# A tile's first four transposes on TensorE, written as two, three matmuls, and two

## The chip, the cores and the metric

The kernel runs on one core of one Trainium2 chip. The metric is the device time of one execution in microseconds; before the change the median of three runs is 2777.08 us (2773.55 to 2779.66).

## The reference

The program is a Fourier filter with soft thresholding, followed by a gated feed-forward block. `x` has 8 sequences of 3072 tokens with 256 features; the feed-forward width is 1536.

```python
X = np.fft.rfft(x, axis=1)
Yr = Xr @ w_r - Xi @ w_i + b_r
Yi = Xr @ w_i + Xi @ w_r + b_i
Yr = np.sign(Yr) * np.maximum(np.abs(Yr) - 0.01, 0.0)   # the same for Yi
y = np.fft.irfft(Yr + 1j * Yi, n=3072, axis=1)
xn = y / sqrt(mean(y * y, -1) + 1e-6) * rms_g           # 24576 tokens
g, val = xn @ w_gate, xn @ w_val
out = (g / (1 + exp(-g)) * val) @ w_out
```

## The kernel before, in words

The 24,576 tokens are cut into 48 tiles T = 0 to 47 of 512 tokens, six tiles to a sequence (a batch b). For each tile there are 12 steps, one per 128 columns of the feed-forward width, 576 steps in all. A step forms the gate and value products of the tile into the PSUM banks `g` and `v` (`straight`, L955, in the first three tiles; `products`, L979, in the other 45), goes through the Silu and the product with the value on ScalarE and VectorE, and adds its share of the output into the bank `acc` (`down`, L1014). Numbers are kept as a high and a low float32r part, so each product is three matmuls (high by high, high by low, low by high). That is why nearly every piece of TensorE's work in `products`, `down` and the Fourier part is three matmuls of 128x256 or a multiple of three; in `straight` it is twelve.

While batch b is worked off, the next sequence is filtered in the same program (`spectrum`): its Fourier units put matmuls into the bank `f` (names `pf`, `pm`, `pb`, L572 to L699), woven in between the steps of three of the tiles.

Before a tile's steps can begin, its 512 normalised tokens have to stand with the features on the partitions. `transposes` (L912) does this for one half h of the features: four TensorE transposes of 128x128 in plain float32 (`pt`, L917), one per 128 tokens, into one PSUM bank, which ScalarE then reads in one instruction (L931, into `xf`). h = 0 comes first and h = 1 some steps later. Both use the pool `f`, which has a single bank, and so do the Fourier units. So a tile has eight transposes, in two runs of four. `combine` then forms the operands of the tile's products on VectorE and ScalarE (L936 to L941).

The order of everything is made by a planner (`Plan`): each operation is recorded with a due time, the engines it can run on, a cost, and the names that it reads and writes (`op`). `schedule` simulates the engines several times forwards and backwards and returns the operations by their start; `emit` (L292) writes them out in that order. Within an engine that order is the program's order; the waits between engines follow from what is read and written. An operation on TensorE is one Python function and was always written out in one piece, though neighbouring operations can come from different steps.

Around one tile's transposes the trace's names are: `pt` the transposes, `acc` the output sums, `g` and `v` the gate and value products, `xf` the transposed tile before it is combined.

Of the kernel before, what the change touches and what calls it, by code (L numbers as in the profile page):

```python
# [127 lines left out]
class Plan:  # L128
# [61 lines left out]
    def schedule(self):  # L190
        ops = self.ordered()
        wrote, read, after = {}, {}, [[] for _ in ops]
        waits = [0] * len(ops)
        for i, (_, _, _, _, rs, ws) in enumerate(ops):

            one = tuple(t for t in rs if t in self.BANKS)
            rs, ws = tuple(t for t in rs if t not in one), ws + one
            deps = {wrote[t] for t in rs + ws if t in wrote} | {j for t in ws for j in read.get(t, ())}
            for j in deps:
                after[j].append(i)  # L200
            waits[i] = len(deps)
            for t in ws:
                wrote[t], read[t] = i, []
            for t in rs:
                read.setdefault(t, []).append(i)
        start, on = self.forward(ops, after, waits, [o[0] for o in ops], None)
        best = None
        for n in range(self.PASSES):
            late = self.backward(ops, after, start, on)
            start, on = self.forward(ops, after, waits, late, None if n % 4 == 3 else on)  # L210
            end = max(start)
            if best is None or end < best[0]:
                best = end, start, on
        _, start, on = best
        return [(ops[i][3], on[i]) for _, i in sorted(zip(start, range(len(ops))))]

    def lag(self, e, to):
        near = 0.0 if e == "P" else 0.06
# [71 lines left out]
        return late  # L290

    def emit(self):  # L292
        for fn, e in self.schedule():
            fn(e)


@with_exitstack
def fourier_glu_kernel(ctx: ExitStack, tc: tile.TileContext, x, w_r, w_i, b_r, b_i, wg, wv, wo, rg, tabs, units, tws, out):
# [3 lines left out]
    P = 128  # L302
# [35 lines left out]
    def f32(ap):  # L338
        return ap.bitcast(F32)
# [7 lines left out]
    def op(engines, cost, fn, r=(), w=()):  # L347
        plan.add(at[0], engines, cost, fn, [*r, *gate], w)

    def dve(n):  # L350
        return 0.09 + n / 990

    def act(n, more=0.0):
        return 0.1 + more + n / 1180
# [16 lines left out]
    class Room:  # L371


        def __init__(self, tag, shape, name, dt=F32):
            pool, n = POOLS[tag]
            k = turns[tag] = turns.get(tag, -1) + 1
            self.ring, self.k, self.n = tag, k, n
            self.tok = Tok(f"{tag}{k % n}")
            self.tok.room = self
            self.first = [self.tok, f"{tag}#"]  # L380
            self.args, self.t = (pool, shape, name, dt, tag), None
# [6 lines left out]
        def __call__(self):  # L388
            if self.t is None:
                pool, shape, name, dt, tag = self.args  # L390
                self.t = pool.tile(list(shape), dt, tag=tag, name=name)
            return self.t

    class Bank(Room):
# [9 lines left out]
        def flat(self):  # L404
            return self().rearrange("p a b -> p (a b)")
# [28 lines left out]
    def first(s, p, n=4, tag="t4"):  # L434
        x0, x1, x2 = ((lambda k=k: blk(s, k)()[:, p:p + n, :]) for k in range(3))
        s0, s1, s2 = (s.tok(*range(8 * k + p, 8 * k + p + n)) for k in range(3))
        t = Room(tag, (P, n, D), f"t4_{s.b}_{p}")
        add(n * D, lambda f: f(t(), x1(), x2(), ALU.add), s1 + s2, t.first)
        add(n * D, lambda f: f(x0(), x0(), t(), ALU.add), [t.tok], s0)

        def diff():
            add(n * D, lambda f: f(x1(), x1(), x2(), ALU.subtract), s2, s1)

        def rest():
            op("V", dve(n * D), lambda _: V.scalar_tensor_tensor(x2(), t(), -1.5, x0(), ALU.mult, ALU.add), [t.tok] + s0, s2)

        return diff, rest
# [464 lines left out]
    def transposes(get, toks, T, h, xn, xf):  # L912
        ps = Room("acc" if T == 0 and h else "f", (P, 4, P), f"pt{T}_{h}")

        def go(_):
            for i in range(4):
                PE.matmul(  # L917
                    ps()[:, i, :], lhsT=get(i)[:, h * P:(h + 1) * P], rhs=ident,
                    start=(i == 0), stop=(i == 3), is_transpose=True, skip_group_check=True,
                )  # L920

        flat = lambda: ps().rearrange("p a b -> p (a b)")
        op("P", 0.45, go, toks, ps.first)
        if xf is None:
            to = lambda lp: xn()[:, lp, 2 * h:2 * h + 2, :].rearrange("p a b -> p (a b)")
            op("A", act(512) + 0.09, lambda _: A.activation(to(0), flat(), AF.Copy, scale=rgs[:, h:h + 1]), [ps.tok, "rgs"], [xn.part(f"h{h}0")] + xn.first * (h == 0))
            w = [xn.part(f"h{h}1")] + ["ready"] * (T == 0 and h)
            op("V", dve(512) + 0.06, lambda _: V.scalar_tensor_tensor(to(1), flat(), rgs[:, h:h + 1], f32(to(0)), ALU.mult, ALU.subtract), [ps.tok, xn.part(f"h{h}0")], w)
            return
        to = lambda: xf()[:, 2 * h:2 * h + 2, :].rearrange("p a b -> p (a b)")  # L930
        op("A", act(512) + 0.09, lambda _: A.activation(to(), flat(), AF.Copy, scale=rgs[:, h:h + 1]), [ps.tok, "rgs"], [xf.tok] + xf.first * (h == 0))  # L931
# [155 lines left out]
    for p, tag in zip((0, 4, 2, 6), ("t4", "as", "xs", "t3")):  # L1087
        rest = first(s, p, 2, tag)
# [72 lines left out]
    for h in range(2):  # L1161
        transposes(lambda i: rows()[:, i, :], [f"{rows.tok}.{p}" for p in range(4)] + [rows.tok, "ident"], 0, h, xns[0], None)
# [110 lines left out]
    for b in range(B):  # L1273
# [6 lines left out]
        for t in range(NT):  # L1280
            T = b * NT + t
            for i in range(NF):
                n = NF * T + i
                if T:
                    at[0] = n - 3
                    if not plain(T):
                        trs[n] = fetch(0, i, Room("tr", (P, 2, 512), f"tr{n}", F32R))
                    else:
                        trs[n] = trs[n - 1] if i % 4 else fetch(2, i // 4, Room("tr", (P, 2, 512), f"tb{n}", F32R))
                    if NF <= n < NF * PLAIN and n % (PLAIN - 1) == 0:  # L1290
                        at[0] = n - 2.9
                        mixed_weights((n - NF) // (PLAIN - 1))
                    at[0] = n - 1
                    wo_s[n] = fetch(1, i, Room("wo", (P, 2, D), f"wo{n}", F32R))
                o = step(n, xns[T], i, not plain(T))
                if i == 0 and T + 1 < NT * B:
                    nb, nt = (b, t + 1) if t + 1 < NT else (b + 1, 0)
                    xns[T + 1] = Room("xn", (P, 2, 7, 256), f"xn{T + 1}", F32R)
                    xf = Room("xf", (P, 7, 256), f"xf{T + 1}") if not plain(T + 1) else None
                    for h in range(2):  # L1300
                        at[0] = NF * (T + 1) - 4 + h
                        transposes(
                            lambda i, nb=nb, nt=nt: seqs[nb]()[:, 4 * nt + i, :],
                            seqs[nb].tok(*range(4 * nt, 4 * nt + 4)), T + 1, h, xns[T + 1], xf,
                        )
                    if xf:
                        combine(T + 1, xns[T + 1], xf)
            at[0] = NF * (T + 1) + LATER - 0.95
            store(b, t, o)
# [31 lines left out]
```

## Time and profile before

| | us |
|---|---|
| median of three runs | 2777.08 |
| profiled execution, its own time | 2773.16 |
| its span, from the first to the last instruction | 2771.4 |
| TensorE matmuls (PE), busy | 2733.7 (99%) |
| weight loads (PEld), busy | 2720.0 (98%) |
| VectorE (DVE), busy | 2330.5 (84%) |
| ScalarE (ACT), busy | 1987.4 (72%) |

A matmul's recorded duration (279 ns) is its way through a pipeline; the next begins before it is done. The pace of TensorE is therefore read as a stretch's length divided by the number of matmuls in it, not from a busy share, which is full either way. A table by windows gives the length, the busy time and the count in brackets for each engine, and the clock that TensorE was granted (1.00 is 2.4 GHz). A window counts an instruction that only reaches into it, so each count is two to three too high.

### The profile page before, as it was taken

To read this page: it belongs to the slowest core of one execution; us is meant where nothing else is said; L and a number is where in the kernel's file an instruction comes from. 1 tells how busy PE (TensorE), PEld (TensorE's weight loads), DVE (VectorE), ACT (ScalarE), POOL (GpSimd) and SP (SyncE) were. 2 spreads that over 40 slices of the span, in tenths; PEclk is the share of its full clock that TensorE was granted. 3 is DMA by queue.
4 is the path that set the end of the run, shared out by engine and by line. 5 is a ranking of instruction groups with operands and counts; after the bars stand their busy time and mean duration, and the time that the engine had idled before them with its cause. 6 is when DMAs were issued, how large, how long until landed. Compare 5 with 4: busy or idle time off the path is not lost.

```text
span 2771.4 us, 60161 instructions
## 1 busy us (share of the span) xinstructions
PE 2733.7 (99%) x23321; PEld 2720.0 (98%) x23321; DVE 2330.5 (84%) x4063; ACT 1987.4 (72%) x4894; POOL 90.4 (3%) x177
## 2 busy tenths in 40 slices
PE   7899999999999999999999999999999999999999
PEld 6799999999999999999999999999999999999999
DVE  9989789987998779987899778997789887966665
ACT  5656678777877778777787777877778777776665
POOL 0000000000000000000000000000000000000000
PEclk9999999999999999999999999999999999999999
DMA  6476676676776667767686666866667666666665
GB/s 223 148 237 211 210 230 227 220 227 214 232 250 218 212 218 244 229 209 229 217 260 213 219 225 210 260 213 218 221 221 253 214 222 218 208 207 219 211 211 189
DMA packets 256112, 610.94 MB, mean 220 GB/s; under 512 B 24401, under 2 KB 81106, under 8 KB 255826
## 3 DMA queue, kind: packets, MB, share of 16 engines
q1 hardware_dynamic: 231634, 519.00, 56.6%
q0 software_dynamic: 24192, 88.09, 10.6%
q8 instruction: 183, 3.00, 0.4%
q14 instruction: 103, 0.84, 0.1%
HBM read 567.68 MB, written 39.32 MB: 219 GB/s over the span
## 4 chain that ended last, share of the span: by engine, by line
PE 97%; DVE 2%; DMA 1%; ACT 1%; issue 0%; SPq 0%; ACTq 0%; DVEq 0%
PE acc L1014 28%; PE v L979 27%; PE g L979 20%; PE pf L572 4%; PE pm L634 4%; PE pb L699 2%; PE pm L630 2%; PE v L955 2%; PE g L955 2%; PE pt L917 2%; PE pm L755 1%; PE pb L694 1%; PE pb L779 1%; PE pm L611 1%; PE pf L733 1%
## 5 line engine op out<-in xcount | busy, mean ns | idle before, releaser
L1014 PE MATMUL acc<-wo,hs 128*128 128x256 f32 x6912 | 1008.7, 279 | 2.2 <-DMA wo<-do 1.4
L1014 PEld LDWEIGHTS acc<-wo,hs 128*128 128x128 f32 x6912 | 891.5, 188 | 3.5 <-DMA wo<-do 1.6
L979 PE MATMUL v<-xn,tr 128*128 128x256 f32 x4860 | 785.4, 279 | 0.7 <-DVE y L992 0.7
L979 PEld LDWEIGHTS v<-xn,tr 128*128 128x128 f32 x4860 | 659.8, 188 | 1.3 <-DVE y L992 1.1
L979 PE MATMUL g<-xn,wb 128*128 128x256 f32 x3240 | 543.2, 279 | 0.8 <-ACT h L993 0.8
L992 DVE TENSOR_TENSOR y<-v,p 128x512 f32<-128x512 f32 x540 | 370.6, 686 | 115.7 <-PE v L979 108.3
L979 PEld LDWEIGHTS g<-xn,wb 128*128 128x128 f32 x3240 | 448.7, 188 | 1.0 <-ACT h L993 1.0
L1007 DVE TENSOR_TENSOR hs<-h,hs 128x512 fp32r<-128x512 f32 x576 | 394.4, 685 | 63.7 <-ACT hs L1006 59.3
L996 DVE TENSOR_TENSOR h<-h,y 128x512 f32<-128x512 f32 x540 | 369.7, 685 | 69.2 <-ACT h L995 66.5
L1006 ACT ACTIVATE hs<-h 128x512 fp32r<-128x512 f32 x576 | 362.1, 629 | 79.2 <-DVE h L996 41.8
L985 ACT ACTIVATE v<-g 128x256 f32<-128x256 f32 x540 | 200.4, 371 | 132.5 <-PE g L979 128.4
L988 ACT ACTIVATE v<-v 128x256 f32<-128x256 f32 x540 | 200.4, 371 | 109.3 <-PE v L979 106.1
L979 PE MATMUL g<-xn,tr 128*128 128x256 f32 x1620 | 276.1, 279 | 0.0
L979 PE MATMUL v<-xn,wb 128*128 128x256 f32 x1620 | 275.5, 279 | 0.0
L995 ACT ACTIVATE h<-v 128x256 f32<-128x256 f32 x540 | 206.5, 382 | 68.9 <-PE v L979 63.7
L993 ACT ACTIVATE h<-g 128x256 f32<-128x256 f32 x540 | 207.0, 383 | 66.8 <-PE g L979 54.2
L979 PEld LDWEIGHTS g<-xn,tr 128*128 128x128 f32 x1620 | 226.6, 188 | 0.0
L979 PEld LDWEIGHTS v<-xn,wb 128*128 128x128 f32 x1620 | 226.5, 188 | 0.0
L545 POOL DMA_DIRECT2D tab<-in_tabs_dram x168 | 89.4, 532 | 2259.6 <-PE v L979 973.4
L986 ACT ACTIVATE p<-g 128x256 f32<-128x256 f32 x296 | 112.7, 381 | 47.1 <-DVE y L992 45.4
L572 PE MATMUL pf<-tab,as 128*128 128x256 f32 x1008 | 137.5, 279 | 1.9 <-ACT as L564 1.5
L572 PEld LDWEIGHTS pf<-tab,as 128*128 128x128 f32 x1008 | 126.0, 189 | 2.3 <-ACT as L564 1.7
(172 smaller groups left out, 3529.8 us busy)
## 6 DMA issues: line engine op xcount, KB each, us to landing
tr<-dt SPq DMA_DIRECT2D x540, 512.0 KB, 4.0
wo<-do SPq DMA_DIRECT2D x564, 256.0 KB, 3.5
tab<-in_tabs_dram POOLq DMA_DIRECT2D x168, 512.0 KB, 4.8
out_dram<-o SPq DMA_DIRECT2D x32, 512.0 KB, 4.4
seq<-in_x_dram SPq DMA_DIRECT2D x28, 512.0 KB, 5.7
seq<-in_x_dram SPq DMA_DIRECT2D x25, 256.0 KB, 4.8
unit<-in_units_dram SPq DMA_DIRECT2D x12, 512.0 KB, 4.3
dt<-tw SPq DMA_DIRECT2D x12, 512.0 KB, 4.0
```

Of the source, the lines that this page charges most:

```text
L572: PE.matmul(ps[:, h, :], lhsT=r()[:, lp, ri, h * P:(h + 1) * P], rhs=f[:, rp, ri, :], start=(h + k + ri == 0), stop=(k == 2 and ri == 1), ...
L979: PE.matmul(dst(), lhsT=w(lp), rhs=xn()[:, rp, x, :], start=start and k == 0, stop=k == 2, skip_group_check=True)
L985: op("A", act(256), lambda _: A.activation(left(), p1(), AF.Copy), [one.tok], two.first)
L986: op("AV", {"A": act(256), "V": dve(256)}, lambda e: A.activation(p5(), p5_(), AF.Copy) if e == "A" else V.tensor_copy(p5(), p5_()), [one. ...
L988: op("A", act(256), lambda _: A.activation(right(), left(), AF.Copy), [], [two.tok])
L992: op("V", dve(512), lambda _: V.tensor_tensor(y(), two(), p5().unsqueeze(1).to_broadcast([P, 2, 256]), ALU.add), [two.tok, p5.tok], y.first)
L993: op("A", act(256), lambda _: A.activation(s()[:, :256], p1(), AF.Silu), [one.tok], s.first)
L995: op("A", act(256), lambda _: A.activation(s()[:, 256:], right(), AF.Silu), [two.tok], [s.part("b")])
L996: op("V", dve(512), lambda _: V.tensor_tensor(s(), s(), y().rearrange("p a b -> p (a b)"), ALU.mult), [y.tok, s.part("b")], [s.tok])
L1006: op("A", act(512), lambda _: A.activation(h()[:, 0], s(), AF.Copy), [s.tok], h.first)
L1007: add(512, lambda f: f(h()[:, 1], s(), f32(h()[:, 0]), ALU.subtract), [s.tok], [h.tok])
L1014: PE.matmul(o()[:, c, :], lhsT=h()[:, lp, c * P:(c + 1) * P], rhs=wo_()[:, rp, :], start=(i == 0 and k == 0 and c % 2 == 0), stop=(i == NF ...
```

## The change

`emit` learns to hold back part of an operation. An operation whose function is a `Halves` is written out as its first half; the rest is kept and written out right after the next TensorE operation, or sooner, if an operation comes up that touches the PSUM bank written, or that writes what the transposes read. `transposes` uses this for h = 0 of every tile but the first. The planner's order, its costs and the engines chosen are not touched; it still plans the four as one operation.

```diff
     def emit(self):
-        for fn, e in self.schedule():
-            fn(e)
+        rest = None
+        for (_, _, _, fn, reads, writes), e in self.schedule():
+            if rest and (rest[2] & {*reads, *writes} or rest[1] & {*writes}):
+                rest = rest[0](e)
+            after = fn(e)
+            if rest and e == "P":
+                rest = rest[0](e)
+            if isinstance(fn, Halves):
+                rest = after, {*reads}, {*writes}
+        assert rest is None
+
+class Halves:
+    def __init__(self, go, n):
+        self.go, self.n = go, n
+
+    def __call__(self, _):
+        self.go(0, self.n // 2)
+        return lambda _: self.go(self.n // 2, self.n)
...
     def transposes(get, toks, T, h, xn, xf):
-        def go(_):
-            for i in range(4):
+        def go(i0, i1):
+            for i in range(i0, i1):
...
-        op("P", 0.45, go, toks, ps.first)
+        op("P", 0.45, Halves(go, 4) if T and not h else lambda _: go(0, 4), toks, ps.first)
```

TensorE's order before, at a tile of the second batch (`pt_0` is h = 0, `pt_1` is h = 1, x is the number of instructions):

```order
L1014 MATMUL acc_5557<-wo_5692,hs_5647 128x256 x6
L917 MATMUL pt_0_5750<-ident,seq_1670 128x128 x4
L979 MATMUL v_5680<-xn_5212,tr_5593 128x256 x3
L979 MATMUL v_5755<-xn_5212,tr_5649 128x256 x3
L1014 MATMUL acc_5557<-wo_5692,hs_5647 128x256 x6
L917 MATMUL pt_1_5782<-ident,seq_1670 128x128 x4
```

The same place after the change (the lines stand 19 further down, and a name's number has moved by two):

```order
L1033 MATMUL acc_5557<-wo_5692,hs_5647 128x256 x6
L936 MATMUL pt_0_5750<-ident,seq_1670 128x128 x2
L998 MATMUL v_5680<-xn_5212,tr_5593 128x256 x3
L936 MATMUL pt_0_5750<-ident,seq_1670 128x128 x2
L998 MATMUL v_5753<-xn_5212,tr_5649 128x256 x3
L1033 MATMUL acc_5557<-wo_5692,hs_5647 128x256 x6
L936 MATMUL pt_1_5782<-ident,seq_1670 128x128 x4
```

One piece of three matmuls has gone ahead of the last two transposes of h = 0. This happens in 47 tiles; in one of them, in `straight`, the piece is twelve matmuls, in the other 46 it is three.

ScalarE's order before, at the same place:

```order
L801 ACTIVATE sq_7_5757,ssq_160<-seq_1670 128x256
L931 ACTIVATE xf_5766<-pt_0_5750,rgs 128x512
L988 ACTIVATE v_5755<-v_5755 128x256
L993 ACTIVATE h_5780<-g_5651 128x256
L1006 ACTIVATE hs_5787<-h_5701 128x512
L931 ACTIVATE xf_5766<-pt_1_5782,rgs 128x512
```

And after the change:

```order
L820 ACTIVATE sq_7_5755,ssq_160<-seq_1670 128x256
L950 ACTIVATE xf_5766<-pt_0_5750,rgs 128x512
L1007 ACTIVATE v_5753<-v_5753 128x256
L1012 ACTIVATE h_5780<-g_5651 128x256
L1025 ACTIVATE hs_5787<-h_5701 128x512
L950 ACTIVATE xf_5766<-pt_1_5782,rgs 128x512
```

Nothing moves on ScalarE, and nothing on VectorE, GpSimd or SyncE either; the first reading of `pt` (L931, now L950) waits for a transpose that stands three matmuls later.

## Rows read from the trace of the kernel before

**Rows 1.** The page: busy time of each engine, and the granted clock in 40 slices.
```profile
PE 2733.7 (99%) x23321; PEld 2720.0 (98%) x23321; DVE 2330.5 (84%) x4063; ACT 1987.4 (72%) x4894; POOL 90.4 (3%) x177
PEclk9999999999999999999999999999999999999999
```

**Rows 2.** The page: the chain that ended last, by engine.
```profile
PE 97%; DVE 2%; DMA 1%; ACT 1%; issue 0%; SPq 0%; ACTq 0%; DVEq 0%
```

**Rows 3.** Waits of PE from 130 us on: total us, times, longest.
```profile
PE pf L572 <- ACT as L564: 1.5, 1, 1.5
PE acc L1014 <- DMA wo<-do: 1.4, 1, 1.4
PE acc L1014 <- ACT o L1028: 0.7, 4, 0.2
```

**Rows 4.** By windows, six tiles: stretch, length, busy and count by engine, PEclk, DMA.
```profile
1443.00:1506.00 63.00, 63.00 (x558) 63.00 (x557) 61.90 (x107) 44.64 (x114) 0.53 (x1) 1.00 0.71 230
1514.00:1575.00 61.00, 61.00 (x521) 61.00 (x520) 49.97 (x84) 42.82 (x100) 3.71 (x7) 1.00 0.68 219
1579.00:1649.00 70.00, 70.00 (x620) 70.00 (x619) 54.60 (x91) 50.94 (x121) 5.30 (x10) 1.00 0.67 221
1653.00:1698.00 45.00, 45.00 (x385) 45.00 (x384) 32.55 (x55) 32.66 (x79) 2.65 (x5) 1.00 0.66 220
1704.00:1731.00 27.00, 27.00 (x231) 27.00 (x230) 26.67 (x44) 19.99 (x53) 0.00 (x0) 1.00 0.62 197
1733.00:1752.00 19.00, 19.00 (x164) 19.00 (x163) 17.85 (x37) 16.50 (x55) 0.00 (x0) 1.00 0.69 226
1754.00:1764.00 10.00, 10.00 (x91) 10.00 (x90) 8.92 (x19) 9.22 (x30) 0.00 (x0) 1.00 0.88 262
1766.00:1775.00 9.00, 9.00 (x78) 9.00 (x78) 8.24 (x20) 8.05 (x24) 0.00 (x0) 1.00 0.91 299
1779.00:1842.00 63.00, 63.00 (x558) 63.00 (x558) 61.90 (x107) 44.39 (x114) 0.53 (x1) 1.00 0.72 234
```

**Rows 5.** By windows, three more stretches.
```profile
1507.00:1513.00 6.00, 6.00 (x55) 6.00 (x55) 5.97 (x11) 4.70 (x11) 0.54 (x1) 1.00 0.58 194
266.00:295.00 29.00, 29.00 (x249) 29.00 (x248) 22.74 (x37) 16.80 (x32) 2.11 (x4) 1.00 0.52 168
298.00:351.00 53.00, 53.00 (x470) 53.00 (x469) 40.40 (x66) 38.77 (x91) 4.24 (x8) 1.00 0.65 205
```

**Rows 6.** TensorE in order of time at 568 us: start, us, what.
```profile
568.28 0.60 PE L917 MATMUL pt<-ident,seq 128*128 128x128 f32 x4
568.63 0.60 PE L1014 MATMUL acc<-wo,hs 128*128 128x256 f32 x3
569.07 0.52 PE L979 MATMUL g<-xn,wb 128*128 128x256 f32 x3
569.42 0.52 PE L979 MATMUL v<-xn,tr 128*128 128x256 f32 x3
```

**Rows 7.** What the trace says of the transposes `pt` on PE.
```profile
L917 PE MATMUL pt<-ident,seq x376: 270/272/273, 142.4 to 2704.4; 128*128 128x128 f32 x188
```

**Rows 8.** TensorE in order of time at 445 us: a tile's two runs, close together.
```profile
445.86 0.60 PE L917 MATMUL pt<-ident,seq 128*128 128x128 f32 x4
447.71 0.60 PE L917 MATMUL pt<-ident,seq 128*128 128x128 f32 x4
```

**Rows 9.** ScalarE in order of time, the same place.
```profile
446.62 0.67 ACT L931 ACTIVATE xf<-pt,rgs 128x512 f32<-128x512 f32 x1
```

**Rows 10.** Who waited for ScalarE's `xf`: engine, tile, line, us, times.
```profile
  DVE xf L936: 5.7, 7
```

**Rows 11.** TensorE in order of time at two of its waits.
```profile
1778.02 0.85 PE L1014 MATMUL acc<-wo,hs 128*128 128x256 f32 x5 [0.18 <-ACT o L1028]
297.44 0.61 PE L1014 MATMUL acc<-wo,hs 128*128 128x256 f32 x3 [1.36 <-DMA wo<-do]
```

More of the change, by code (lines that the diff above doesn't have):

```diff
@@ L214, in schedule @@
         _, start, on = best
-        return [(ops[i][3], on[i]) for _, i in sorted(zip(start, range(len(ops))))]
+        return [(ops[i], on[i]) for _, i in sorted(zip(start, range(len(ops))))]
     def lag(self, e, to):
```

## The prediction

> **What bounds the kernel now.** I read the page first, then the chain, TensorE's waits, a table by windows, and single stretches in order of time. The page has TensorE busy for 99% of the span, the chain runs through it for 97%, and its longest single wait after 130 us is 1.5 us [rows 1 to 3]. So only two things can change the time: how long TensorE's own instructions take, and a new wait on it.
>
> The table by windows shows what the page hides. TensorE is full in every window and its clock is 1.00, the level of 2.4 GHz, in every window, yet it has two paces [rows 4]. From 1579 to 1649 us there are 620 matmuls in 70 us. Less the two or three that only reach into the window that is 113.3 ns each; 1443 to 1506 and 1779 to 1842 give the same, 558 in 63 us. From 1514 to 1575 it is 521 in 61 us, or 117.6 ns, and so for 385 in 45 us and 231 in 27 us. I call them the fast and the slow pace; 4.3 ns, or 3.7%, lie between them. The work is alike on both sides and the clock is equal, so the pace is a state in which the stream of weight loads and matmuls finds itself. The windows are cut at the transposes: each of the nine ends where a tile's run of four stands, or where TensorE waited.
>
> Two things switch the pace. One is a run of transposes. Where one run stands between windows, the paces are slow (1704 to 1731), slow (1733 to 1752), fast (1754 to 1764), slow (1766 to 1775) [rows 4]: a cycle of three, fast, slow, slow, with one step to a run. Where both runs of a tile stand between windows (1514, 1579, 1653, 1704), the cycle takes two steps: slow, fast, slow, slow. The other is a wait. After 1.36 us for a weight at 297 us the stream goes from slow (249 in 29 us) to fast (470 in 53 us) [rows 5, 11]; after 0.18 us at 1778 us from slow (78 in 9 us) to fast [rows 4, 11]. The first run behind such a wait keeps it fast: 55 in 6 us between the runs at 1506 and 1513 us [rows 5].
>
> So two runs a tile send the long stretches round the cycle, two of three slow. The change makes it three runs a tile, two of them short.
>
> **The change part by part.** *The transposes themselves.* Their number stays; 376 of them stand in the tiles 1 to 47 [rows 7], and half of those, 188, are in the runs that are cut. From the first of four to the second piece behind them is 0.79 us (568.28 to 569.07), of which three matmuls at 117.6 ns are 0.353, so a run costs 0.437 us, or 109 ns a transpose with both its ends [rows 6]. Inside the run the four start 0.33 us apart from first to last (0.60 less the 0.272 of one), 0.11 each, so the ends cost between -0.02 and +0.03 us. One run more in each of 47 tiles is -0.9 to +1.4 us. I take +0.6, a little above the middle, since at 568.63 the first three matmuls behind the run take 0.60 where the next three take 0.52.
>
> *The three matmuls that go ahead.* They start 0.22 us earlier (two transposes of 109 ns), so a wait of theirs shows by up to 0.22 us more. They stood right behind the four before, without a wait in the timeline at 568 us; I take zero, and the bound is 47 x 0.22 = 10 us if none of them has any slack.
>
> *The reader of the bank.* ScalarE's reading of h = 0 can start 0.35 us later (three matmuls). It is hidden where ScalarE comes to it later anyway. The tightest place that I found is at 445 us: the two runs start 1.85 us apart, the reading starts 0.76 us after its run's start, and ends at 447.29, 0.42 us ahead of the run that needs the bank again [rows 8, 9]. With 0.35 us less, 0.07 us are left, and if it fails, a wait of a few tenths appears. VectorE waited for `xf` 5.7 us in all 7 times [rows 10] and is not what the end hangs on. I take 0; the bound is 47 x 0.35 = 16 us. No DMA and no queue of SyncE or GpSimd is moved.
>
> *The pace.* This is where a large term can come from, and the trace of before holds no run of two. If a run counts as a step whatever its length, three runs a tile close the cycle: the long stretch behind the second four of one tile has the pace of that behind the last, until a wait resets it. Take one batch from the second wait to the next, 1443 to 1779 us [rows 4]. Its long slow windows are 61 + 45 + 27 = 133 us; at the fast pace they are 3.7% shorter, 4.9 us. The short stretches between a tile's first and second transposes, which are then two steps on, are slow; those that were fast (6 us at 1507 [rows 5] and about 4 us between the windows that end at 1698 and begin at 1704) lose 0.4 us. That is 4.5 us for six tiles, and 47 tiles have 7.8 times that: -35 us. With +0.6 the profiled execution goes from 2773.2 to 2738.8; the median of the runs shown is 3.9 us above the profiled one, so 2743 us. If the short stretches run fast too, the windows at 1733 and 1766 us (28 us) add 1.0 us a batch, and the edges left out of the windows about 0.6, so 2727 is the least that I can work out; the range goes to 2724.
>
> [...] Rows 4 show two paces at one clock. [...]
>
> **The rivals.** *B, held in a slow pace.* A closed cycle can keep a slow stretch as well as a fast one. For it: behind a wait the first run keeps the stream fast, and if the half runs count like runs, the tile's third step then lands in the second slow place, where each further tile leaves it. Against it: each wait makes the stream fast again, and no wait that I found leaves it slow for long, so a slow hold is broken in every batch while a fast one, once reached, is not. The price: the long fast windows that no wait made, 70 + 10 us a batch, become 3.8% longer, 3.0 us, and the short ones 0.4; 7.8 times 3.4 is +27, so 2801 for the execution and 2805 us for the median. It decides from the tile at which the cycle closes. If the 63 us behind the wait turn slow too, 2.4 us a batch more, 2824.
>
> *C, two halves make one step.* If what moves the stream is the number of transposes and not the ends of a run, two halves move it as far as four did, and the tile still makes two steps. For it: the four together are passed in an even 0.11 us each, so the step could build up along them. Against it: that the whole effect shows as one jump of the pace at the run's end [rows 6]. Time: 2773.8, or 2778 us for the median, and a few us either way where a stretch's place in the cycle moves.
>
> *D, the halves hold in some batches alone*, for instance where the Fourier units' waits fall differently: about half of the gain, 2760, or half of B's loss, 2791.
>
> **How the numbers follow.** My forecast A has 0.48, B 0.20, C 0.23, D 0.09. A is ahead of B because waits push one way only; I cannot read from the trace what a run of two does, and the chances say so. The predicted time is A's, 2743; its own range is 2724 to 2755. The range for all reaches over C to 2790 and leaves out nearly all of B. About 0.2% (5.5 us) is what a measurement of this kernel can tell from no change. Faster takes A, half of D and 0.04 of C: 0.56. The same takes 0.13 of C and 0.01 of D: 0.14. Slower takes B, the rest of C (0.06: a reading of the bank that comes late, or stretches that change places) and of D (0.04): 0.30.
>
> **What would show it.** In a table by windows of the changed kernel, cut at the transposes, A shows some 113 ns in nearly every long stretch, from tile to tile without the change of two to three; B shows 117.6 in them; C shows the same alternation as now. The span's clock stays 1.00 throughout. A run of two should cost 0.22 us in the timeline, 0.44 for both, as four do now. If TensorE's waits grew by more than 3 us in total, at `pt` of h = 1 or at a Fourier unit's `pf`, the reader of the bank was not hidden. I am wrong in the main point if the long stretches keep alternating, or are all slow.

## The result, and the profile after

The changed kernel takes 2730.72 us (median of 4 runs, 2729.29 to 2732.48), the kernel before 2776.82 us on the same chip (4 runs). The ratio is 0.9835, with a 95% interval of 0.9818 to 0.9852: faster, by 46 us. The prediction was 2743 us. The profiled execution took 2732.48 us, that of before 2773.16 us, so 40.7 us less.

First the page after: busy time by engine, the granted clock in 40 slices, and the chain.

```profile
PE 2691.1 (99%) x23321; PEld 2677.0 (98%) x23321; DVE 2322.7 (85%) x4063; ACT 1980.8 (73%) x4894; POOL 90.3 (3%) x177
PEclk9999999999999999999999999999999999999999
PE 97%; DVE 2%; DMA 1%; ACT 0%; issue 0%; SPq 0%; ACTq 0%; DVEq 0%
```

The number of instructions is that of before, and TensorE is as full as before, but it is busy 42.6 us less (2733.7 in [rows 1]). So the same instructions took less time. The table by windows says how. It shows the batch that [rows 4] show before: stretch, length, busy time and count by engine, granted clock, DMA.

```profile
1424.00:1487.00 63.00, 63.00 (x559) 63.00 (x557) 61.90 (x107) 44.70 (x115) 0.53 (x1) 1.00 0.71 231
1496.00:1554.00 58.00, 58.00 (x514) 58.00 (x513) 48.66 (x83) 41.59 (x99) 3.70 (x7) 1.00 0.71 226
1558.00:1628.00 70.00, 70.00 (x620) 70.00 (x620) 54.59 (x91) 50.94 (x121) 5.29 (x10) 1.00 0.71 221
1632.00:1675.00 43.00, 43.00 (x382) 43.00 (x381) 32.21 (x54) 32.38 (x78) 2.66 (x5) 1.00 0.68 230
1681.00:1708.00 27.00, 27.00 (x241) 27.00 (x240) 26.97 (x45) 20.43 (x55) 0.00 (x0) 1.00 0.64 204
1710.00:1728.00 18.00, 18.00 (x161) 18.00 (x160) 17.27 (x38) 16.06 (x54) 0.00 (x0) 1.00 0.74 233
1730.00:1740.00 10.00, 10.00 (x91) 10.00 (x90) 8.98 (x18) 9.21 (x29) 0.00 (x0) 1.00 0.89 284
1742.00:1751.00 9.00, 9.00 (x79) 9.00 (x78) 8.28 (x20) 8.18 (x25) 0.00 (x0) 1.00 0.85 282
```

A long stretch here is one from a tile's second four to the next tile's first transposes, a short one lies between a tile's first transposes and its second four. The windows of 58, 43 and 27 us, long stretches, answer to those of 61, 45 and 27 us, which were slow. Now 514 matmuls stand in 58 us, 382 in 43 and 241 in 27; less the two or three that only reach into the window, some 113.3 ns each. All long stretches of this batch are fast. Of the two short ones in the table (1710 and 1742 us) the second is slow (79 in 9 us). From the end of one wait to the end of the next the batch takes 330.0 us (1423.64 to 1753.62) where it took 335.7 (1442.31 to 1778.02): 5.7 us less.

The waits hardly grew: from 130 us on TensorE's sum to 7.8 us, where they summed to 6.3. The lines show four of the eight after the change (total, times, longest); the third is new, the others stand in [rows 3] as they were before.

```profile
PE pf L591 <- ACT as L583: 1.6, 1, 1.6
PE acc L1033 <- DMA wo<-do: 1.2, 1, 1.2
PE pm L630 <- DVE xs L621: 1.1, 1, 1.1
PE acc L1033 <- ACT o L1047: 0.9, 4, 0.2
```

VectorE's waits for `xf`, which answer to [rows 10], are the same too: 5.6 us in 7 times.

```profile
  ACT xf L950: 5.6, 7
```

What did grow is ScalarE's own wait for the transposes, since the last two come three matmuls later. Who waited for `pt` (engine, tile, line, us, times), before and after:

```profile
  ACT xf L931: 2.8, 5
  ACT xf L950: 10.0, 22
```

None of TensorE's waits is at `pt`, and those at the Fourier units' `pf` are as long as before within 0.1 us, so these 7 us stayed on ScalarE.

The cut itself stands in TensorE's order of time at 1487 us: start, duration, what.

```profile
1487.68 0.38 PE L936 MATMUL pt<-ident,seq 128*128 128x128 f32 x2
1487.82 0.60 PE L998 MATMUL g<-xn,wb 128*128 128x256 f32 x3
1488.26 0.38 PE L936 MATMUL pt<-ident,seq 128*128 128x128 f32 x2
1488.39 0.60 PE L998 MATMUL g<-xn,tr 128*128 128x256 f32 x3
1488.83 0.74 PE L998 MATMUL v<-xn,tr 128*128 128x256 f32 x5
```

From 1487.68 to 1488.26 it is 0.58 us for two transposes and three matmuls, of which 0.34 are matmuls at the fast pace; from 1488.26 to 1488.83 it is 0.57. So the halves cost 0.24 and 0.23 us, together 0.47 where four in one run cost 0.437 [rows 6].

### The profile page after: what moved, and what is told of

It reads as the page before. It is cut to its first block, busy times and chain, and to the rows that moved or that the text cites. A ratio compares the mean times of both kernels' runs of the same rounds, so it can differ in the third digit from the quotient of the medians.

```text
span 2730.7 us, 60153 instructions
## 1 busy us (share of the span) xinstructions
PE 2691.1 (99%) x23321; PEld 2677.0 (98%) x23321; DVE 2322.7 (85%) x4063; ACT 1980.8 (73%) x4894; POOL 90.3 (3%) x177
## 4 chain that ended last, share of the span: by engine, by line
PE 97%; DVE 2%; DMA 1%; ACT 0%; issue 0%; SPq 0%; ACTq 0%; DVEq 0%
PE acc L1033 28%; PE v L998 27%; PE g L998 20%; PE pf L591 4%; PE pm L653 4%; PE pb L718 2%; PE pm L649 2%; PE v L974 2%; PE g L974 2%; PE pt L936 2%; PE pm L774 1%; PE pb L713 1%; PE pf L752 1%; PE pb L798 1%; PE pm L630 1%; PE pb L695 0%
## 5 line engine op out<-in xcount | busy, mean ns | idle before, releaser
L1033 PE MATMUL acc<-wo,hs 128*128 128x256 f32 x6912 | 998.6, 277 | 2.1 <-DMA wo<-do 1.2
L1033 PEld LDWEIGHTS acc<-wo,hs 128*128 128x128 f32 x6912 | 881.0, 188 | 3.6 <-ACT o L1047 1.6
L998 PE MATMUL v<-xn,tr 128*128 128x256 f32 x4860 | 776.6, 277 | 0.6 <-DVE y L1011 0.6
L998 PEld LDWEIGHTS v<-xn,tr 128*128 128x128 f32 x4860 | 652.6, 188 | 1.3 <-DVE y L1011 1.0
L998 PE MATMUL g<-xn,wb 128*128 128x256 f32 x3240 | 537.3, 277 | 0.9 <-ACT h L1012 0.9
L1026 DVE TENSOR_TENSOR hs<-h,hs 128x512 fp32r<-128x512 f32 x576 | 396.4, 688 | 57.8 <-ACT hs L1025 52.8
```

Of the source, the lines that this page charges most:

```text
L998: PE.matmul(dst(), lhsT=w(lp), rhs=xn()[:, rp, x, :], start=start and k == 0, stop=k == 2, skip_group_check=True)
L1026: add(512, lambda f: f(h()[:, 1], s(), f32(h()[:, 0]), ALU.subtract), [s.tok], [h.tok])
L1033: PE.matmul(o()[:, c, :], lhsT=h()[:, lp, c * P:(c + 1) * P], rhs=wo_()[:, rp, :], start=(i == 0 and k == 0 and c % 2 == 0), stop=(i == NF ...
```

## The experiments

What had to be explained was not that the pace changed, but why a cut in half holds the fast one. Twelve kernels vary the transposes of the 47 tiles. In what follows "2,2 | 4" means: the first four transposes in two runs of two with a piece of TensorE's work between them, the second four in one run. Before is 4 | 4. Cuts are written by a class that takes the place of `Halves`, and `emit` asks it for its parts until none is left (not shown). The diffs below are extracts, against the changed kernel; where no `op` line is shown and the text says nothing else, the runs are not cut, as in 6 | 6:

```diff
-class Halves:
...
+class Parts:
+    def __init__(self, go, *cuts):
+        self.go, self.cuts = go, cuts
+
+    def __call__(self, _, k=0):
+        self.go(self.cuts[k], self.cuts[k + 1])
+        if k + 2 < len(self.cuts):
+            return lambda _: self(_, k + 1)
```

### Only the matmuls go ahead: 3 matmuls, 4 | 4

```diff
-        op("P", 0.45, Halves(go, 4) if T and not h else lambda _: go(0, 4), toks, ps.first)
+        op("P", 0.45, Parts(go, 0, 0, 4) if T and not h else lambda _: go(0, 4), toks, ps.first)
```

> The next piece of three matmuls goes ahead of all four transposes of h = 0, which stay in one run; nothing is split. My theory (the number of runs in a tile decides the pace behind them): two runs a tile as before, so the long stretches alternate between 113 and 117.6 ns a matmul, ratio to before 0.997 to 1.003. Rival (the three matmuls that start 0.22 us earlier bring the gain, or the later reading of the bank does): as the changed kernel, 0.983.

Measured: 1.0012 (1.0001 to 1.0022). By windows of TensorE alone (stretch, length, busy and count, granted clock, DMA) long stretches still change from tile to tile:

```profile
1585.00:1656.00 71.00, 71.00 (x606) 1.00 0.67 216
1662.00:1703.00 41.00, 41.00 (x364) 1.00 0.67 225
```

71 us over 604 is 117.5 ns and 41 us over 362 is 113.3. Work put ahead of the whole run brings nothing; so what the changed kernel gains comes of the cut in the run.

### Only the second four cut: 4 | 2,2

```diff
+        op("P", 0.45, Parts(go, 0, 2, 4) if T and h else lambda _: go(0, 4), toks, ps.first)
```

> Only the second four (h = 1) are split in two and two, the first four stay in one run. Theory (runs): three runs a tile again, so the long stretches keep one pace from tile to tile; fast, as a wait leaves it: 0.980 to 0.988; a hold in the slow pace would show as 1.01 and as 117.6 ns in nearly every long stretch. Rival (number of transposes): eight a tile as before, so they alternate, 0.997 to 1.003.

Measured: 0.9987 (0.9974 to 0.9999). Three runs a tile, two of them short, as in the changed kernel, and yet the long stretches are mostly slow:

```profile
1518.00:1575.00 57.00, 57.00 (x487) 1.00 0.68 219
1582.00:1652.00 70.00, 70.00 (x597) 1.00 0.68 219
1659.00:1700.00 41.00, 41.00 (x364) 1.00 0.66 224
```

117.5 and 117.6 ns in the first two, 113.3 in the third. That three runs a tile hold the fast pace is refuted here: which of the fours is cut matters.

### Both cut: 2,2 | 2,2

```diff
+        op("P", 0.45, Parts(go, 0, 2, 4) if T else lambda _: go(0, 4), toks, ps.first)
```

> Both fours are split in two and two, four runs a tile. Theory (runs, three steps close the cycle): four runs are one step too many, so the long stretches go round the cycle again, one fast to two slow: 0.996 to 1.004. Rival (any split helps, by mixing transposes with matmuls): at least the changed kernel's gain, 0.983 or less. Rival (number of transposes): alternates as before.

Measured: 1.0036 (1.0024 to 1.0048), a little slower than before. Nearly every long stretch is slow from tile to tile, which is what the prediction's rival B described for the changed kernel:

```profile
1518.00:1575.00 57.00, 57.00 (x486) 1.00 0.68 219
1582.00:1652.00 70.00, 70.00 (x597) 1.00 0.68 219
1659.00:1702.00 43.00, 43.00 (x367) 1.00 0.66 214
1710.00:1735.00 25.00, 25.00 (x214) 1.00 0.59 191
```

### Longer runs: 6 | 6

Two of the four transposes are made twice, so a run has six; the output is unchanged.

```diff
-            for i in range(i0, i1):
+            for n, i in enumerate((2, 3, 0, 1, 2, 3) if T and i1 else range(i0, i1)):
...
+        op("P", 0.45, lambda _: go(0, 4), toks, ps.first)
```

> Each run of four in tiles 1 to 47 becomes one run of six: two transposes are made twice, the doubles first. 188 transposes more at 109 ns are 20.5 us (+0.74%). Theory (runs): two runs a tile, so the long stretches alternate as before: ratio 1.005 to 1.010. Rival (number of transposes, in a cycle of three): six is a whole turn, so each run leaves the pace as it was, and the long stretches hold one pace: 0.991 if that is the fast one, 1.018 if the slow one.

Measured: 0.9904 (0.9889 to 0.9919), with 188 transposes (20.5 us) more than before. Two runs a tile, and they hold the fast pace: 497 in 56 us and 603 in 68.

```profile
1506.00:1562.00 56.00, 56.00 (x497) 1.00 0.72 224
1568.00:1636.00 68.00, 68.00 (x603) 1.00 0.70 225
```

So a run is not one step whatever its length. Since six is twice three, a second rule was open: steps go by the number of transposes, modulo three.

### Four and five, five and five: 4 | 5 and 5 | 5

```diff
+            for n, i in enumerate((3, 0, 1, 2, 3) if T and i1 and h else range(i0, i1)):
```

The second kernel has it without `and h`. The transpose of i = 3 is made twice.

> The tile's first four transposes are one run of four, as before; of the second four the first is made twice (into the same place, output unchanged), so that this run has five. Added work: 47 transposes at 109 ns, 5.1 us, 0.18%. Theory 'the number of transposes counts, modulo three, where TensorE has settled between the runs': four is one step, five is two, a tile closes the cycle, so one pace holds over the long stretches: held fast 0.985 to 0.988 (as six_each, 0.990, with 15 us less work), held slow 1.010 to 1.014. Rival 'a run is a step, whatever its length': two runs a tile, the long stretches alternate as before, 1.001 to 1.004.

> Both runs of a tile have five transposes, the first of each made twice. Added work: 94 transposes at 109 ns, 10.2 us, 0.37%. Theory 'number modulo three': two steps and two steps are four, one more than a whole turn, so the long stretches go through all three states from tile to tile as before: 1.002 to 1.007. Rival 'a run that is longer than four leaves the fast pace' (which six_each could mean as well): 0.985 to 0.990.

Measured: 0.9851 (0.9836 to 0.9866) and 0.9856 (0.9842 to 0.9871). For 4 | 5 the rule of three gave that. For 5 | 5 it gave an alternation, but the stretches of 5 | 5 show none: long and short ones alike are fast (the fifth row is a short one):

```profile
1502.00:1558.00 56.00, 56.00 (x497) 1.00 0.72 230
1565.00:1633.00 68.00, 68.00 (x603) 1.00 0.70 225
1639.00:1680.00 41.00, 41.00 (x364) 1.00 0.67 223
1688.00:1713.00 25.00, 25.00 (x223) 1.00 0.61 196
1717.00:1733.00 16.00, 16.00 (x144) 1.00 0.72 219
```

The rule of three has fallen too; its rival, that a run longer than four leaves the fast pace alone, agrees with 5 | 5 and 6 | 6.

### The halves further apart: 2, more work, 2 | 4

```diff
+        op("P", 0.45, Parts(go, 0, 2, 2, 2, 4) if T and not h else lambda _: go(0, 4), toks, ps.first)
```

> The changed kernel with the two halves of the first four further apart: up to three pieces of TensorE's work between them (mostly six matmuls, some three, nine or twelve) in place of one (three matmuls). Same instructions, no added work. Theory 'number modulo three, where TensorE has settled between the runs; three matmuls are too few to settle': with a longer gap the halves are runs of their own, 2+2+4 = 8, two more than whole turns, the long stretches alternate: 0.997 to 1.003. Rival 'three runs of any length close the cycle' : 0.982 to 0.987, as the changed kernel.

Measured: 0.9844 (0.9828 to 0.9861), as the changed kernel. In 22 of the 47 tiles six matmuls stand between the halves, in 17 three as before and in 8 nine or twelve; the distance made no difference.

### Other cuts: 3,1 | 4, then 1,3 | 4, then 1,1,2 | 4

```diff
+        op("P", 0.45, Parts(go, 0, 3, 4) if T and not h else lambda _: go(0, 4), toks, ps.first)
...
+        op("P", 0.45, Parts(go, 0, 1, 4) if T and not h else lambda _: go(0, 4), toks, ps.first)
...
+        op("P", 0.45, Parts(go, 0, 1, 2, 4) if T and not h else lambda _: go(0, 4), toks, ps.first)
```

> The changed kernel with the first four cut after the third transpose, not the second: three, three matmuls, one; the second four in one run. Same instructions as the changed kernel. Theory 'number modulo three': three is a whole turn and does nothing, one and the four are a step each, two steps a tile as before, the long stretches alternate: 0.997 to 1.003. Rival 'three runs close the cycle': 0.982 to 0.987.

> The changed kernel with the first four cut after the first transpose: one, three matmuls, three; the second four in one run. Same instructions as the changed kernel. Two rules have fallen by now: a run is a step whatever its length (two cut runs a tile did not hold), and steps go by the number of transposes modulo three (two runs of five held the fast pace). What is left: any first part that isn't a lone run of four, followed by one run of four, holds the fast pace: 0.982 to 0.988. Rival: what the cut does depends on its parts, so that another cut need not hold: with three of the four transposes in one run, as in the cut after the third (0.987), more stretches stay slow, 0.986 to 1.000.

> The changed kernel with the first four in three parts: one, one, two, with three matmuls between them where the next use of the bank leaves room (in 29 of 47 tiles; one and three in the other 18); the second four in one run. Same instructions, four runs a tile. If any cut first part followed by one run of four holds the fast pace: 0.980 to 0.988. If it is the count of runs that holds (three a tile), four runs a tile don't close it: as with both fours cut in two, 1.000 to 1.004.

Measured: 0.9865 (0.9851 to 0.9880), 1.0001 (0.9991 to 1.0011) and 0.9894 (0.9877 to 0.9910). The first two have the same instructions and the same three runs a tile, and lie 1.4% apart. In 3,1 | 4 the long stretches are fast, and the short ones mostly slow (the second row, 147 in 17 us):

```profile
1503.00:1559.00 56.00, 56.00 (x497) 1.00 0.72 228
1717.00:1734.00 17.00, 17.00 (x147) 1.00 0.68 214
```

In 1,3 | 4 the long stretches alternate as before, one in three fast (first and fourth row):

```profile
1517.00:1573.00 56.00, 56.00 (x496) 1.00 0.72 229
1579.00:1650.00 71.00, 71.00 (x605) 1.00 0.66 216
1656.00:1699.00 43.00, 43.00 (x367) 1.00 0.66 215
1707.00:1732.00 25.00, 25.00 (x223) 1.00 0.63 195
```

So the prediction's count of runs does not decide it. That a cut first part holds the fast pace, whatever its parts, misses for 1,3 | 4; that it depends on the parts stands. That four runs a tile do not hold misses too: 1,1,2 | 4, with four runs in 29 of its tiles, is mostly fast.

### A narrow fifth transpose: 4 | 5 and 2,2 | 5

```diff
-            for i in range(i0, i1):
+            for n, i in enumerate((3, 0, 1, 2, 3) if T and i1 and h else range(i0, i1)):
+                w = 32 if T and h and n == 0 else P
...
-                    ps()[:, i, :], lhsT=get(i)[:, h * P:(h + 1) * P], rhs=ident,
+                    ps()[:, i, :w], lhsT=get(i)[:w, h * P:(h + 1) * P], rhs=ident[:w, :w],
```

The second kernel keeps the changed kernel's cut of the first four.

> As the kernel with runs of four and five, but the extra, fifth transpose of the second run is narrow: 32 rows of the same data, 32 columns, written ahead of the fourth's own result and replaced by it (output unchanged). It streams 32 columns in place of 128, so the run lasts longer than a run of four by less than 109 ns; how much less the trace will tell. Theory 'the number of transposes in a run decides what it does to the pace': as four and five (0.9851), less up to 47 x 82 ns = 3.8 us: 0.982 to 0.987. Rival 'the length in time of the interruption decides': a run hardly longer than four acts as a run of four, the long stretches alternate as before: 0.997 to 1.003.

> The changed kernel (first four cut into two and two) with the narrow extra transpose in the second run as well (output unchanged). Meant as the fastest version: in the changed kernel some 230 us still run at the slow pace (8.5 us to be had at most), and runs of five left nothing slow outside a few stretches behind waits. If the run of five keeps or makes the fast pace here too: slow time under 150 us and 0.981 to 0.984, against 0.9835 of the changed kernel. If a run of five behind two runs of two acts otherwise than a run of four does: 0.985 to 1.003.

Measured: 0.9919 (0.9905 to 0.9933) and 0.9937 (0.9924 to 0.9950). The first lies in neither range and cannot tell the two theories apart: the narrow transpose made the run longer than a full one does, not shorter. The second misses what it was meant for (473 us at the slow pace, where under 150 were expected) and lies in its rival's range, in good part for the narrow transposes' own time. TensorE in order of time with the narrow one (start, us, what):

```profile
1504.84 0.39 PE L1037 MATMUL acc<-wo,hs 128*128 128x256 f32 x2
1505.15 0.83 PE L940 MATMUL pt<-ident,seq 32*128 32x32 f32 x5
1505.74 0.60 PE L1002 MATMUL v<-xn,tr 128*128 128x256 f32 x3
1506.17 0.50 PE L1002 MATMUL g<-xn,wb 128*128 128x256 f32 x3
```

The same with a full fifth transpose, in 4 | 5:

```profile
1557.27 0.51 PE L1001 MATMUL g<-xn,wb 128*128 128x256 f32 x3
1557.61 0.71 PE L939 MATMUL pt<-ident,seq 128*128 128x128 f32 x5
1558.08 0.60 PE L1001 MATMUL g<-xn,tr 128*128 128x256 f32 x3
1558.51 0.52 PE L1001 MATMUL v<-xn,tr 128*128 128x256 f32 x3
```

From 1504.84 to 1506.17 it is 1.33 us with five matmuls, so 0.76 for the run; from 1557.27 to 1558.51 it is 1.24 us with six, so 0.56. Whether the number of transposes or the time of the run decides stays open. 2,2 | 5, meant as the fastest version, is not. Of all versions none is shown to be faster than the changed kernel.

### The account over all kernels

In each trace the time from one matmul's start to the next was summed over the intervals of 116 to 120 ns, from 130 us on: the time at the slow pace. At the fast pace it would be 3.77% shorter (113.33 to 117.78 ns). The last column is the span less that share and less the work added (109 ns a transpose).

| kernel | ratio | span us | at slow pace us | share to be had us | added us | left us |
|---|---|---|---|---|---|---|
| before, 4 \| 4 | 1 | 2771.4 | 1390 | 52.5 | | 2718.9 |
| changed, 2,2 \| 4 | 0.9835 | 2730.7 | 228 | 8.6 | | 2722.1 |
| 3 matmuls, 4 \| 4 | 1.0012 | 2779.6 | 1578 | 59.5 | | 2720.1 |
| 4 \| 2,2 | 0.9987 | 2775.8 | 1531 | 57.8 | | 2718.0 |
| 2,2 \| 2,2 | 1.0036 | 2787.5 | 1749 | 66.0 | | 2721.5 |
| 6 \| 6 | 0.9904 | 2751.0 | 239 | 9.0 | 20.5 | 2721.5 |
| 4 \| 5 | 0.9851 | 2733.7 | 148 | 5.6 | 5.1 | 2723.0 |
| 5 \| 5 | 0.9856 | 2737.5 | 161 | 6.1 | 10.2 | 2721.2 |
| halves apart | 0.9844 | 2729.9 | 228 | 8.6 | | 2721.3 |
| 3,1 \| 4 | 0.9865 | 2740.8 | 535 | 20.2 | | 2720.6 |
| 1,3 \| 4 | 1.0001 | 2772.9 | 1393 | 52.6 | | 2720.3 |
| 1,1,2 \| 4 | 0.9894 | 2745.6 | 631 | 23.8 | | 2721.8 |
| 4 \| narrow 5 | 0.9919 | 2751.3 | 392 | 14.8 | not known | 2736.5 |
| 2,2 \| narrow 5 | 0.9937 | 2754.0 | 473 | 17.8 | not known | 2736.2 |

Twelve kernels whose spans lie 58 us apart come out within 5 us of each other. To within these 5 us the share at the slow pace makes their differences. The two narrow ones lie some 15 us above; 47 transposes at 0.32 us (0.76 less the 0.44 of four) are 15.0 us.

## Why the prediction was right, and where it was wrong

**The bound and its two paces: right.** TensorE is busy for 99% before and after, its waits grew by 1.5 us in all, and the account shows that the time hangs on how much of the stream runs at the slow pace.

**The halves' ends: +0.6 us predicted, about 1.4 measured** (0.47 less 0.44 us in one place, by 47), the upper bound. The account leaves 3.2 us for all that is not pace (2722.1 less 2718.9). The waits' 1.5 us would be most of the rest, but this is not shown, since the kernels scatter by as much.

**Matmuls ahead and the reader of the bank: zero, right.** No wait of TensorE at `pt` appeared and VectorE waited for `xf` as before; the later reading shows in ScalarE's 7 us, which cost nothing. Three matmuls ahead of a whole run changed hardly anything (1.0012).

**The pace term: the sign right, the size too small.** -35 us was predicted; the slow time fell by 1162 us, which by 3.77% is 43.9 us. The term's mis-sized part is the short stretches, which the prediction turned slow. In every other tile they are fast: 1710 to 1728 us holds 161 in 18 us where 1733 to 1752 was slow [rows 4], 0.7 us a batch. Of the two fast ones that were to lose 0.4 us, the one of 6 us stayed fast and only the one of about 4 us turned slow (1677.35 to 1677.71 us holds three matmuls), so some 0.1 was lost. That is 1.0 of the 1.2 us between 4.5 and 5.7; the rest lies in the edges that the windows left out, less what the halves cost. The measured execution thus lies between the two sums of the prediction, all short stretches slow and all fast. Of the 12 us between 2743 and 2730.7, 6 are this (9 gained, less some 3 of other cost) and 6 the step to the median: I added the 3.9 us by which the execution before lay under its median, and the one after lay 1.8 above.

**"One run is one step", the reason given: wrong.** It named the outcome, and the long stretches are held fast as it said, but three runs a tile do not hold in 4 | 2,2 or 1,3 | 4, and two do in 5 | 5. That the sign came out right is therefore luck in good part. What the cases show is only that each arrangement sends the long stretches, between waits, into a pattern of its own: nearly all fast, nearly all slow, or a change from tile to tile. The pace ahead of a run does not tell what a run does either. Counted over all tiles from the matmuls' starts on both sides of a run, four transposes behind a fast stretch left the pace fast in 8 of 39 cases before (6 of the 8 in the first run behind a wait, as the prediction read it), in 24 of 24 after, and in 44 of 44 in 4 | 5; five behind a fast stretch left it fast in 89 of 90 in 5 | 5. So the stream has more states than two paces. What they are, and why this cut holds the fast pace, stays open.

**"Each wait makes the stream fast again", said against rival B: wrong as a rule.** In 4 | 5 a wait of 1.59 us for a weight leaves a fast stream slow for 54 us; in the kernel before a wait of 1.36 us at the same weight did the opposite [rows 5, 11]. TensorE by windows ahead of it and behind it, and between them the wait in order of time:

```profile
270.00:294.00 24.00, 24.00 (x214) 1.00 0.60 193
296.33 0.62 PE L1036 MATMUL acc<-wo,hs 128*128 128x256 f32 x3 [1.59 <-DMA wo<-do]
297.00:351.00 54.00, 54.00 (x461) 1.00 0.64 201
```

In the changed kernel, too, a fast stream turns slow between two windows, without a run of transposes between them, and stays so for 53 us:

```profile
745.00:771.00 26.00, 26.00 (x231) 26.00 (x231) 23.26 (x44) 23.45 (x67) 0.00 (x0) 1.00 0.95 318
775.00:828.00 53.00, 53.00 (x451) 53.00 (x451) 51.27 (x92) 35.24 (x87) 0.53 (x1) 1.00 0.63 209
```

**The rivals.** B, a hold in the slow pace, is a thing that happens, in 2,2 | 2,2; that it was not the changed kernel's fate could not be read from the trace before. C, that two halves are one step, is refuted for the changed kernel by its windows; D, a hold in some batches alone, by the 228 us that are left at the slow pace in the whole span. The range (2724 to 2790) and the chance of 0.56 for faster reflected that the direction could not be derived, which the experiments bear out: neighbours of the change, 1,3 | 4 and 2,2 | 2,2, bring nothing or a loss.

**Two paces at one clock.** Every kernel here shows both 113.3 and 117.8 ns at a granted clock of 1.00. The Trainium skill ("TensorE: Matmul & The Clock Gate", section "Back-to-back issue gap") gives an isolated matmul N/2.4 + 2.5 ns at full clock, for 256 columns an estimate of 109 ns, and says that in a stream of weight loads and matmuls both set the spacing. The runs agree in that neither pace is 109 ns, and there are as many weight loads as matmuls here (23321 each, [rows 1]); what each of them has to do with the two paces no run shows.

## What to carry to other kernels

Where an engine is full, divide its windows by their instruction counts: a stream can have two paces at one clock, and then a few per cent lie in what interrupts it, not in its work. How runs of interrupting instructions are cut was worth 1.65% here, but neither the sign nor the size could be derived from the trace that did not hold the cut: try several (which four, where, a run longer) and compare the slow time, not the order. Check the story with an account as above: the span less the pace's share and the added work should be the same for all.

## What the runs showed of the hardware

- The stream of 128x128 weights and 256 columns has two paces, 113.33 and 117.78 ns from start to start, both held for hundreds of matmuls at a granted clock of 1.00 (603 in 68 us in 5 | 5, 606 in 71 us with three matmuls ahead).
- More work can take less time: 5 | 5 makes two transposes a tile more than before, 10.2 us in all, and its median is 38.8 us lower (2736.48 against 2775.23).
- A transpose of 32 rows and 32 columns at the head of a run of full ones cost 0.32 us in the place shown, three times the 0.109 us of a full one, and the account of the two kernels that have it agrees (15 us for 47).
- A wait can turn the stream from fast to slow as well as from slow to fast: 1.59 us at 296 us in 4 | 5, 1.36 us at 297 us before.
